# Causal attention and top-1 MoE on one core: the V loads of the first group are put at later places in the load queue

## The chip, the cores and the metric

The kernel runs on one NeuronCore of a Trainium2 chip. The metric is the device time of one execution in microseconds. The median of three runs of the kernel before is 532.28 us (532.24 to 537.39). The engines named below are TensorE (PE in the rows, PEld for its weight loads), VectorE (DVE), ScalarE (ACT), GpSimd (POOL) and SyncE (SP), which here issues all the loads that matter.

## What is computed

Attention with a memory over B=4, H=8, S=576, D=64, then a mixture of experts with one expert for each token (2304 tokens of 512, 8 experts, hidden size 1024).

```python
scores = np.where(causal, -1e9, q @ k.T / sqrt(D))
local  = softmax(scores) @ v
mem    = einsum('bhsd,bhde->bhse', phi(q), M_prev) / (phi(q) . z_prev + 1e-06)
x      = g * mem + (1 - g) * local            # g = sigmoid(beta), x is 2304 x 512
e      = argmax(normalize(x) @ normalize(expert_emb).T / tau)
out    = gate * (relu(x @ w1[e]) @ w2[e])
```

## The kernel before

**Tiling.** The attention is done in 8 groups: batch b and one half of the heads (4 heads), group 0 being batch 0, heads 0 to 3. The 576 rows of a group are four full tiles of 128 and a tail of 64, so there are query tiles i = 0 to 4 and key blocks 0 to 4 (the last one is the tail). Query tile i reads the key blocks 0 to i. A query tile of a group is worked in units of one or more heads: scores on TensorE (L692), maximum and mask on VectorE (L703), exponent on ScalarE (L731), transposes of the result on TensorE (L740) into the tiles aT0 to aT3 by a copy (L752, L754), then the product with V on TensorE (L767, function sC). Ahead of the scores stand the transposes of q and k (L604, L563, L634) and their split into two parts (L613, L622). L852 multiplies phi(q) with the memory, whose matrices M and normalisers z are loaded into Mb (L534, L535). Fillers (L272) are matmuls on an identity that the kernel places in waits of TensorE.

The second half is the mixture of experts: L1505 is its first product, L1518 transposes the hidden values, L1522 (ScalarE) and L1526 (VectorE) split them, L1532 is the second product, L1545 moves its result. L1491 transposes gathered rows of x and L1495 moves them. L1358 to L1371 load weights.

**What sets the order.** Nearly all work is handed to a list scheduler (class Sched) as operations with a name, an engine, a modelled duration, the operations that it depends on, and a priority; a lower number goes first. The scheduler plays the engines and the DMA transfers in modelled time and picks on each engine, among operations that can start at about the same modelled time, the one with the lowest priority number. The program is written in the order of the modelled starts, and on the chip each engine runs its list in order. Real waits come from semaphores that are derived from the tiles which an instruction reads and writes, so an instruction waits for all that it touches, whether or not the scheduler's list of dependences has it.

**The loads.** All loads of q, k, V, M and z are issued by SP in one queue. q and k of group 0 have the priorities 0.3 n for tile n (k 0.1 lower, the tail counts as n = 4), those of group 1 1.5 (k 1.4), M and z of batch 0 1.2. Each tile of q, k or V is one load of 128 rows by 4 heads by 64 floats, 131,072 bytes; a tail is half of that. The V rows of group 0 go into the tile VN0, one load for each key block (function load_v, L519, operation `("lv", 0, n)`). VN is a tile of [128, 5 blocks, 4 heads, 65]: 64 values and a one for each head. Its constant parts are written by POOL (L322 to L324).

**The product with V.** For the query tiles 0 to 3, sC takes for each head 128 columns from the flat tile:

```python
c = VW * kb + (D + 1) * hh
nc.tensor.matmul(
    lt[:, P * hh : P * hh + P], u["aT"][:, P * y : P * y + P], vt[:, c : c + P], start=kb == 0, stop=kb == i
)
```

VW is 4 x 65 = 260 columns, a key block. The columns that head hh reads begin at 65 hh and are 128 wide; those behind the 65 of the head are not used afterwards. The list of dependences of this operation (L822 to L824) holds `("lv", gi, kb)` for kb up to i, and for i = 3 also block 4.

Of the kernel before, what the change touches and what calls it, by code (L numbers as in the profile page):

```python
# [39 lines left out]
class Sched:  # L40
# [12 lines left out]
    def op(self, name, eng, dur=0, fn=None, deps=(), prio=0.0, alloc=(), free=(), xfer=None, at=0.0, late=0):  # L53
        alts = eng if isinstance(eng, list) else [(eng, dur, fn)]
        o = dict(name=name, alts=alts, deps=deps, prio=prio, alloc=alloc, free=free, xfer=xfer, n=len(self.ops), at=at, late=late)
        assert name not in self.byname, name
        self.byname[name] = o
        self.ops.append(o)
        for key in free:
            self.nrel[key] = self.nrel.get(key, 0) + 1  # L60
# [115 lines left out]
def kernel(  # L176
# [21 lines left out]
    SP = S + P - TAIL  # L198
# [8 lines left out]
    cfg = PRIO  # L207
# [12 lines left out]
    op, SL = sc.op, sc.slot  # L220
# [80 lines left out]
    def ub(gi):  # L301
        return UB[max(gi, 0)]
# [208 lines left out]
    def load_v(gi):  # L511
        b, g = groups[gi]
        key = ("VN", gi)
        names = []
        for n in range(NFULL + 1):
            r = P if n < NFULL else TAIL

            def f(n=n, r=r):
                nc.sync.dma_start(  # L519
                    VN[SL[key]][0:r, n, :, 0:D], v[b, 4 * g : 4 * g + 4, P * n : P * n + r, :].rearrange("h p d -> p h d")  # L520
                )

            op(("lv", gi, n), "SP", 450, f, (("lva", gi),), (0.4 + 0.3 * n if gi == 0 else ub(gi - 1) + cfg.get("lv", 3.0)),
               xfer=728 * r // P)
        op(("lva", gi), "NOP", 0, None, (), (0.8 if gi == 0 else ub(gi - 1) + cfg.get("lv", 3.0)),
           alloc=(("VN", key),), at=0.0)
# [1117 lines left out]
    for gi in range(NG):  # L1644
        load_v(gi)
        prep_group(gi)
# [172 lines left out]
```

## Time and profile before

| what | us |
|---|---|
| median of the runs | 532.28 |
| the profiled execution | 533.08 |
| its span, first to last instruction | 531.4 |
| TensorE busy in the span | 509.9 (96%) |
| VectorE busy | 309.5 (58%) |
| ScalarE busy | 321.2 (60%) |
| TensorE idle from 0 to 35 us | 4.99 |

The span is 1.7 us shorter than the execution's time. The granted clock of TensorE is 0.995 of full speed on average. Times in the rows count from the start of the span. In a timeline a row is a run of like instructions: its start, the time from the start of its first to the end of its last one, the engine, the line, the operation, the tiles (out<-in), and in brackets the idle time of the engine before it with what ended it. "SPq" and "ACTq" are the queues of SP and ScalarE; a row of SPq is the issuing of a load, not its transfer. TensorE works through a float32 matmul in several passes, so the trace can count more instructions than the order shows. The table's last line is the sum of the idle parts of the seven 5-us windows up to 35 us.

### The profile page before, as it was taken

What the parts mean: (1) busy time and instruction counts of PE and PEld (TensorE: products, weight loads), DVE (VectorE), ACT (ScalarE), POOL (GpSimd) and SP (SyncE); (2) the same over time, 40 slices, a digit from 0 to 9 for tenths busy, and PEclk for the clock granted to TensorE, in tenths of its full rate; (3) what the DMA queues carried; (4) which work ended last, traced back from release to release, by engine and by line L of the source; (5) the groups of instructions that cost most, each with busy time, mean ns of one, the idle gap of its engine ahead of it and who ended that gap; (6) DMA issues with size and microseconds to landing.
All of it is one profiled execution on the core that took longest, in us unless ns stands there. A gap on an engine that the chain in (4) does not pass through costs nothing. (4 is left out here: it accounts for less than half of the span.)

```text
span 531.4 us, 11427 instructions
## 1 busy us (share of the span) xinstructions
PE 509.9 (96%) x3506; PEld 439.7 (83%) x3506; DVE 309.5 (58%) x1003; ACT 321.2 (60%) x627; POOL 191.6 (36%) x266
## 2 busy tenths in 40 slices
PE   7899999999999999999997999999999999999991
PEld 6789998898899999988775888888888888888871
DVE  5677787777877877788981223411157514554540
ACT  5787876678877877687622353532367535664550
POOL 7211524434433433348437222232233332223320
PEclk9999999999999999999999999999999999999997
DMA  6657845135642311376418837542268863787340
GB/s 156 144 79 160 188 102 129 34 82 127 141 108 47 81 41 41 80 264 155 99 13 241 279 85 218 166 114 60 61 218 259 247 174 92 254 292 202 80 79 19
DMA packets 127471, 71.94 MB, mean 135 GB/s; under 512 B 111384, under 2 KB 111512, under 8 KB 127394
## 3 DMA queue, kind: packets, MB, share of 16 engines
q1 hardware_dynamic: 122242, 59.49, 43.1%
q0 software_dynamic: 5152, 11.57, 7.2%
q8 instruction: 30, 0.49, 0.5%
q14 instruction: 47, 0.39, 0.3%
HBM read 111.74 MB, written 10.67 MB: 230 GB/s over the span
## 5 line engine op out<-in xcount | busy, mean ns | idle before, releaser
L1505 PE MATMUL aux<-RB 128*128 128x512 f32 x528 | 126.0, 391 | 3.8 <-ACTq L1457 2.9
L1532 PE MATMUL L<-RC,hhl 128*128 128x512 f32 x528 | 129.1, 394 | 0.1
L1505 PEld LDWEIGHTS aux<-RB 128*128 128x128 f32 x528 | 98.3, 188 | 24.9 <-ACTq L1457 3.1
L1532 PEld LDWEIGHTS L<-RC,hhl 128*128 128x128 f32 x528 | 97.5, 188 | 19.9 <-ACT RC L1389 0.5
L1526 DVE TENSOR_TENSOR hhl<-aux,hhl 128x512 fp32r<-128x512 f32 x45 | 30.9, 690 | 118.1 <-ACTq L1457 58.9
L767 PE MATMUL L<-VN,aT 128*128 128x128 f32 x640 | 87.3, 276 | 0.0
L767 PEld LDWEIGHTS L<-VN,aT 128*128 128x128 f32 x640 | 78.9, 191 | 2.0 <-DVE aT L754 1.1
L1522 ACT ACTIVATE hhl<-aux 128x512 fp32r<-128x512 f32 x45 | 26.7, 598 | 77.2 <-PE aux L1518 40.7
L703 DVE CUSTOM_DVE_ANT_0 a<-aux,mask 128x128 f32<-128x128 f32 (+3 forms) x144 | 62.3, 452 | 12.9 <-PE aux L692 7.9
L731 ACT ACTIVATE a<-a,nb 128x128 f32<-128x128 f32 (+3 forms) x128 | 65.2, 557 | 1.7 <-DVE nb L703 1.2
L740 PE MATMUL aux<-ident,a 128*128 128x128 f32 x384 | 61.8, 278 | 1.5 <-ACT a L731 1.4
L1442 POOL DMA_INDIRECT a<-x_dram,ix x26 | 29.9, 1152 | 85.0 <-DMA ix<-id_dram 72.2
L752 ACT ACTIVATE aT<-aux 128x512 f32<-128x512 f32 (+3 forms) x89 | 44.6, 513 | 26.3 <-PE aux L740 23.7
L919 POOL TENSOR_TENSOR A<-ms,dd 128x256 f32<-128x256 f32 x32 | 20.7, 646 | 90.0 <-DVE dd L903 55.5
L740 PEld LDWEIGHTS aux<-ident,a 128*128 128x128 f32 x384 | 43.5, 141 | 10.1 <-ACT a L731 3.5
L1558 POOL DMA_INDIRECT out_dram<-ys,ix x21 | 22.3, 1064 | 78.3 <-ACTq L1457 55.3
L1514 ACT ACTIVATE hs<-aux 128x512 f32<-128x512 f32 x44 | 23.9, 595 | 36.1 <-PE aux L1505 35.5
L1393 DVE TENSOR_TENSOR RB<-RA,RB 128x1024 fp32r<-128x1024 f32 x24 | 28.4, 1223 | 12.2 <-ACT RB L1389 10.8
L1393 DVE TENSOR_TENSOR RC<-RA,RC 128x1024 fp32r<-128x1024 f32 x24 | 28.5, 1224 | 5.2 <-ACT RC L1389 5.0
L1449 POOL DMA_INDIRECT gg<-gate_dram,ix x23 | 25.8, 1121 | 7.0 <-issue 7.0
L852 PE MATMUL aux<-Mb,qp 128*128 128x130 f32 x160 | 25.1, 279 | 1.9 <-DMA Mb<-in_z_prev_dram 1.9
L925 POOL TENSOR_TENSOR X<-A,Xl 128x256 f32<-128x256 f32 x32 | 24.3, 760 | 5.5 <-DVE Xl L913 2.9
(259 smaller groups left out, 764.2 us busy)
## 6 DMA issues: line engine op xcount, KB each, us to landing
RA<-in_moe_w_dram SPq DMA_DIRECT2D x78, 1024.0 KB
RA<-in_moe_w_dram SPq DMA_DIRECT2D x16, 512.0 KB
RA<-in_k_dram SPq DMA_DIRECT2D x32, 128.0 KB
RA<-in_q_dram SPq DMA_DIRECT2D x32, 128.0 KB
VN<-in_v_dram SPq DMA_DIRECT2D x32, 128.0 KB
x_dram<-x SPq DMA_DIRECT2D x16, 256.0 KB
RA<-in_k_dram SPq DMA_DIRECT2D x8, 64.0 KB
RA<-in_q_dram SPq DMA_DIRECT2D x8, 64.0 KB
```

Of the source, the lines that this page charges most:

```text
L703: nc.vector.tensor_tensor_reduce(out=o, in0=i0, in1=i1, op0=ALU.add, op1=ALU.min, scale=-0.125, scalar=init, accum_out=acc)
L731: nc.scalar.activation(out=a[:, c], in_=a[:, c], func=AF.Exp, scale=-1.0, bias=nb[:, y : y + 1])
L740: nc.tensor.transpose(ps[:, P * y : P * y + P], a[:, P * y : P * y + P], ident)
L752: nc.scalar.activation(out=u["aT"][0:r, o : o + n], in_=t[0:r, 0:n], func=AF.Copy)
L767: nc.tensor.matmul(lt[:, P * hh : P * hh + P], u["aT"][:, P * y : P * y + P], vt[:, c : c + P], start=kb == 0, stop=kb == i)
L1393: nc.vector.tensor_tensor(l, s, h.bitcast(F32), op=ALU.subtract)
L1442: nc.gpsimd.indirect_dma_start(out=xg, out_offset=None, in_=x_dram[0:rows, :], in_offset=bass.IndirectOffsetOnAxis(ap=ix[:, 0:1].bitcast(U ...
L1449: nc.gpsimd.indirect_dma_start(out=gg, out_offset=None, in_=gate_dram[:, :], in_offset=bass.IndirectOffsetOnAxis(ap=G[i]["ix"][:, 1:2].bit ...
L1505: nc.tensor.matmul(G[i]["hp"][n], a[:, cc], w[:, c, 512 * n : 512 * n + 512], start=c == 0 and a is xh and w is w1h, stop=c == KD - 1 and ...
L1522: nc.scalar.activation(out=big("hhl")[n][:, 0:512], in_=G[i]["gps", n], func=AF.Copy)
L1526: nc.vector.tensor_tensor(t[:, 512:1024], G[i]["gps", n], t[:, 0:512].bitcast(F32), op=ALU.subtract)
L1532: nc.tensor.matmul(G[i]["yp"], t[:, cc : cc + P], w[:, c, :], start=c == 0 and a == 0 and w is w2h, stop=c == KF - 1 and a == 1)
```

## The change

The priority of the V loads of group 0 goes from 0.4 + 0.3 n to 0.8 + 0.3 n; all other groups' are as before, and no other line differs.

```diff
-            op(("lv", gi, n), "SP", 450, f, (("lva", gi),), (0.4 + 0.3 * n if gi == 0 else ub(gi - 1) + cfg.get("lv", 3.0)),
+            op(("lv", gi, n), "SP", 450, f, (("lva", gi),), (0.8 + 0.3 * n if gi == 0 else ub(gi - 1) + cfg.get("lv", 3.0)),
                xfer=728 * r // P)
```

Since the scheduler's modelled times move with it, the order of all engines changes in places. On SP, at the start of the queue, the rows stood so before (VN0 is the V tile of group 0, RA holds q and k, bet is beta):

```order
4 L501 DMA RA_80<-in_k_dram 128x4x64
5 L501 DMA RA_80<-in_q_dram 128x4x64
6 L519 DMA VN0_86<-in_v_dram 128x4x64
7 L501 DMA RA_80<-in_k_dram 128x4x64
8 L501 DMA RA_80<-in_q_dram 128x4x64
9 L519 DMA VN0_86<-in_v_dram 128x4x64
10 L501 DMA RA_80<-in_k_dram 128x4x64
11 L501 DMA RA_80<-in_q_dram 128x4x64
12 L519 DMA VN0_86<-in_v_dram 128x4x64
13 L501 DMA RA_80<-in_k_dram 128x4x64
```

and in the changed kernel:

```order
4 L501 DMA RA_80<-in_k_dram 128x4x64
5 L501 DMA RA_80<-in_q_dram 128x4x64
6 L501 DMA RA_80<-in_k_dram 128x4x64
7 L501 DMA RA_80<-in_q_dram 128x4x64
8 L501 DMA RA_80<-in_k_dram 128x4x64
9 L519 DMA VN0_86<-in_v_dram 128x4x64
10 L501 DMA RA_80<-in_q_dram 128x4x64
11 L501 DMA RA_80<-in_k_dram 64x4x64
12 L519 DMA VN0_86<-in_v_dram 128x4x64
13 L501 DMA RA_80<-in_k_dram 128x4x64
```

The first V load has moved from row 6 to row 9, the second from 9 to 12, and the third has left this stretch. Further down SP's queue, from the last load of z for batch 0 on, the changed kernel has these rows (a row with x4 is four loads; en and ta are the experts' embeddings and tau; the row with 64x4x64 ahead of an x4 is the tail of group 1):

```order
21 L535 DMA Mb0_93<-in_z_prev_dram 64x4x1
22 L501 DMA RA_80<-in_k_dram 128x4x64
23 L501 DMA RA_80<-in_q_dram 128x4x64
24 L451 DMA en_145<-in_moe_expert_emb_dram 8x512
25 L452 DMA ta_147<-in_moe_tau_dram 128x1
26 L501 DMA RA_80<-in_k_dram 128x4x64
27 L501 DMA RA_80<-in_q_dram 128x4x64
28 L501 DMA RA_80<-in_k_dram 64x4x64
29 L501 DMA RA_80<-in_k_dram 128x4x64 x4
30 L519 DMA VN0_86<-in_v_dram 128x4x64
31 L501 DMA RA_80<-in_q_dram 64x4x64
32 L501 DMA RA_80<-in_q_dram 128x4x64 x4
```

Row 30 is the third V load, the rows 33 and 34 behind these the fourth and the tail. Before, the last load of z was row 22, the fourth V load row 27, group 1's q tail row 32 and the V tail row 34.

On TensorE, around L852 of group 0, the rows stood so before (L_439 is the result tile of query tile 1 of group 0, VN0 its V, aT2 and aT3 the transposed scores of its two units, each of two heads and two key blocks):

```order
118 L852 MATMUL aux_431<-Mb0_93,qp0_84 128x130 x2
119 L767 MATMUL L_439<-VN0_86,aT2_91 128x128 x4
120 L740 MATMUL aux_451<-ident_71,a_377 128x128 x4
121 L740 MATMUL aux_460<-ident_71,a_399 128x128 x3
122 L740 MATMUL aux_469<-ident_71,a_423 128x128 x3
123 L852 MATMUL aux_479<-Mb0_93,qp0_84 128x130 x2
124 L740 MATMUL aux_485<-ident_71,a_434 128x128 x3
125 L767 MATMUL L_439<-VN0_86,aT3_92 128x128 x4
126 L563 MATMUL aux_509<-ident_71,RA_80 128x64 x4
```

and in the changed kernel, where the result tile is L_441:

```order
112 L852 MATMUL aux_425<-Mb0_93,qp0_84 128x130 x2
113 L740 MATMUL aux_433<-ident_71,a_376 128x128 x4
114 L767 MATMUL L_441<-VN0_86,aT2_91 128x128 x4
115 L740 MATMUL aux_456<-ident_71,a_399 128x128 x3
116 L740 MATMUL aux_462<-ident_71,a_419 128x128 x3
117 L767 MATMUL L_441<-VN0_86,aT3_92 128x128 x4
118 L563 MATMUL aux_484<-ident_71,RA_80 128x64 x4
119 L852 MATMUL aux_491<-Mb0_93,qp0_84 128x130 x2
120 L740 MATMUL aux_499<-ident_71,a_430 128x128 x3
```

The second product of query tile 1 with V (aT3) has moved ahead of the second L852 and of three L740. Ahead of the fourth k and q tile's L604 there were 16, 8, 3 and 6 fillers; now there are 16, 8 and 6.

On TensorE at the place where the attention's last work has ended and the experts' products go on, before the gathered rows (a) are first transposed by L1491, the rows stood so before:

```order
869 L1532 MATMUL L<-RC,hhl 128x512 x18
870 L1505 MATMUL aux<-RB 128x512 x12
871 L1518 MATMUL aux<-ident,hs 128x128 x8
872 L1505 MATMUL aux<-RB 128x512 x12
873 L1532 MATMUL L<-RC,hhl 128x512 x24
874 L1505 MATMUL aux<-RB 128x512 x6
875 L1491 LDWEIGHTS a
```

and in the changed kernel, where eight fillers (L272) stand ahead of the first of these rows and L1532 x18 and L1505 x6 ahead of the fillers:

```order
880 L272 MATMUL aux<-ident_76 128x128
881 L1518 MATMUL aux<-ident,hs 128x128 x8
882 L1505 MATMUL aux<-RB 128x512 x6
883 L1532 MATMUL L<-RC,hhl 128x512 x24
884 L1505 MATMUL aux<-RB 128x512 x18
885 L1491 LDWEIGHTS a
```

Six of the L1505 ahead of L1518 and six of those behind it have moved: six stand ahead of L1518 now, six behind it, and eighteen behind L1532. The aux tiles of the six behind L1518 are in the changed order the PSUM banks that L1518 wrote.

## Rows read from the trace of the kernel before

**Rows 1.** Busy us by stretch (instructions), TensorE's granted clock, DMA share, GB/s

```profile
5.00:10.00 5.00, 4.88 (x47) 3.85 (x46) 2.98 (x11) 2.92 (x8) 4.44 (x25) 1.00 0.82 185
10.00:15.00 5.00, 4.84 (x40) 3.82 (x40) 4.70 (x21) 4.66 (x14) 1.49 (x13) 1.00 0.69 147
15.00:20.00 5.00, 3.07 (x28) 2.64 (x27) 1.23 (x6) 2.68 (x7) 0.00 (x0) 1.00 0.65 140
35.00:240.00 205.00, 204.93 (x1874) 185.82 (x1873) 160.04 (x665) 158.74 (x363) 79.79 (x110) 1.00 0.45 108
```

**Rows 2.** TensorE's longest waits: us in total, times, longest

```profile
PE aux L1505 <- ACTq L1457: 2.9, 1, 2.9
PE aux L272 <- DVE ident L230: 2.5, 1, 2.5
PE aux L852 <- DMA Mb<-in_z_prev_dram: 1.9, 1, 1.9
```

**Rows 3.** SP's longest wait from 0 to 45 us

```profile
SPq L519 <- POOL VN L324: 1.2, 1, 1.2
```

**Rows 4.** Timeline of SP, 0 to 34 us

```profile
1.87 0.50 SPq L404 DMA_DIRECT2D bet<-in_beta_dram  x1
...
2.89 0.51 SPq L501 DMA_DIRECT2D RA<-in_q_dram  x1
4.61 0.37 SPq L519 DMA_DIRECT2D VN<-in_v_dram  x1
...
12.14 0.60 SPq L534 DMA_DIRECT2D Mb<-in_M_prev_dram  x1
...
13.45 1.46 SPq L534 DMA_DIRECT2D Mb<-in_M_prev_dram  x1
14.95 0.62 SPq L535 DMA_DIRECT2D Mb<-in_z_prev_dram  x1
...
22.38 3.33 SPq L501 DMA_DIRECT2D RA<-in_q_dram  x5
```

**Rows 5.** Timeline of TensorE, 12 to 34 us

```profile
12.85 0.71 PE L767 MATMUL L<-VN,aT 128*128 128x128 f32 x4
...
14.38 1.50 PE L692 MATMUL aux<-RB 64*128 64x384 f32 x12
17.80 0.69 PE L852 MATMUL aux<-Mb,qp 128*128 128x130 f32 x4 [1.93 <-DMA Mb<-in_z_prev_dram]
18.33 1.05 PE L767 MATMUL L<-VN,aT 128*128 128x128 f32 x8
19.22 1.26 PE L740 MATMUL aux<-ident,a 128*128 128x128 f32 x10
20.48 0.71 PE L852 MATMUL aux<-Mb,qp 128*128 128x130 f32 x4
21.03 0.49 PE L740 MATMUL aux<-ident,a 128*128 128x128 f32 x3
...
22.34 0.46 PE L563 MATMUL aux<-ident,RA 64*128 64x64 f32 x4
```

**Rows 6.** Timeline of ScalarE: the first use of beta

```profile
4.55 0.21 ACT L338 ACTIVATE invg<-bet 128x8 f32<-128x8 f32 x1 [2.45 <-DMA bet<-in_beta_dram]
```

**Rows 7.** Timeline of all engines, 268 to 290 us

```profile
272.50 1.66 PE L1505 MATMUL aux<-RB 128*128 128x512 f32 x6 [0.46 <-ACT hs L1514]
...
273.99 1.03 PE L1518 MATMUL aux<-ident,hs 128*128 128x128 f32 x8
274.63 1.09 ACT L1522 ACTIVATE hhl<-aux 128x512 fp32r<-128x512 f32 x2 [1.69 <-PE aux L1518]
...
275.26 0.69 DVE L1526 TENSOR_TENSOR hhl<-aux,hhl 128x512 fp32r<-128x512 f32 x1 [2.02 <-ACT hhl L1522]
...
284.42 0.62 PE L1491 MATMUL aux<-ident,a 128*128 128x128 f16 x8
...
286.81 0.60 ACT L1495 ACTIVATE RB<-aux 128x512 fp32r<-128x512 f16 x1 [2.40 <-remote]
```

## The prediction

> **What bounds the kernel now.** I read the busy time by stretch first. From 35 to 240 us TensorE is busy 204.93 of 205 us [rows 1]: whatever comes late before 35 us is carried to the end, and nothing in that stretch can be saved by earlier loads. So only places where TensorE stands still can gain or lose. The list of TensorE's waits names them [rows 2]: 2.5 us for the identity at the start, which no load touches, 1.9 us in front of L852 for the memory normaliser z, 2.9 us near 288 us. The one SP wait that the diff can touch is 1.2 us: the first V load stands behind the memset of VN by POOL (L324), and all loads stand behind it [rows 3].
>
> The queue of SP then shows how tightly the start is packed [rows 4]. The first V load begins at 4.61, the first M load at 12.14, the last z load at 14.95, the tail of group 1's q at 22.38. TensorE's own rows [rows 5] show that it ends twelve L692 at 15.88 (14.38 + 1.50) and starts L852 at 17.80, which is the 1.93 us.
>
> **The change part by part.** SP's order: V block 0 goes from sixth to ninth place, block 1 from ninth to twelfth, block 2 from twelfth to behind the k loads of group 1, block 3 and the tail behind its q loads.
>
> 1. *The wait for the memset goes.* k2 and q2 now stand where V0 was. q1 starts at 2.89 [rows 4], so the next starts at about 3.4 and V0 at about 5.1, after the memset: 1.2 us of queue are won.
>
> 2. *z comes earlier.* Before, 13 loads (V0 to the tail of group 0's q) take 4.61 to 12.14, 0.58 each; two loads ahead of them take 1.87 to 2.89, 0.51 each [rows 4]. After, 12 loads lie between q1 and M, so M starts at 3.4 + 12 x 0.58 = 10.4 (9.5 with 0.51). Then M, z, M, z: before, the last z started 2.81 behind the first M, of which the second M took 1.46; no row says why, so without its excess the step is 1.95. The last z: 11.5 to 13.2, I take 12.6. From issue to use z took 17.80 - 14.95 = 2.85 us, so L852 may go at 14.4 to 16.1, and TensorE gets there at about 15.9. The 1.93 us go, all but 0.2 at worst. **Taken alone: minus 1.9.**
>
> 3. *V block 2 comes too late.* L767 reads 128 columns of V for each head at a pitch of 65, so the fourth head reaches 63 columns into the next key block. The last of the four L767 with aT3 in the changed order (tile L_441) therefore reads V block 2, though query tile 1 multiplies only key blocks 0 and 1. The scheduler's dependences have block 2 only for query tile 2. Before, block 2 was the twelfth load and no L767 waited. After, it is the twelfth load behind the last z. Before, thirteen loads behind the last z took 14.95 to 22.38 [rows 4], so twelve are 6.86 us: V2 starts at 12.6 + 6.86 = 19.5 (18.4 to 20.1).
> Issue to use has no row for V at this place. The nearest: beta's took 4.55 - 1.87 = 2.68 us [rows 4, 6] and z's 2.85, both small; 131,072 bytes at the 185 GB/s of 5 to 10 us [rows 1] add 0.7 at most. So 2.7 to 3.5; I take 3.0, nearer the small ones, because the DMA engines were only 0.65 busy at 15 to 20 us [rows 1]. V2 can be used at 22.5 (21.1 to 23.6).
> When does TensorE want it? The trace counts eight L767 and four L852 where the order has four and two. From 15.9, by [rows 5]: L852 0.53 (17.80 to 18.33), four L740 0.50 (1.26 for ten), L767 0.89 (18.33 to 19.22), six L740 0.76, three quarters of the next L767 0.67: 19.25. **TensorE stands 3.2 us (1.8 to 4.3) where it stood 1.93 before.**
> The balance is made at one common point, the end of this L767 group: 22.34 before, with the second L852 (0.55) and three L740 (0.33) of the rows at 20.48 and 21.03 already done; after, these two come behind it. Loss = 22.5 + 0.25 (the last quarter) + 0.88 - 22.34 = **+1.3 us** (-0.1 to +2.4). Step 2's gain is already in it.
> The Trainium skill, DMA: Bandwidth & Descriptors, section "Anatomy of one DMA", gives 2.0 us plus bytes over 436 GB/s for a DMA of the gpsimd path. By that an estimate for V2 is 2.3 us, 0.7 less than mine, and the loss would be 0.6. The trace does not agree: z needed 2.85 us for 1 KB in all, from SP.
>
> 4. *V blocks 0, 1, 3 and the tail.* V0 starts at 5.1 instead of 4.61 and V1 three loads later, at 6.8; with 3.5 us both are there before 10.5, and the first L767 began at 12.85 [rows 5]. V3 starts six loads behind V2, at 22.9, and is there before 26.5; what reads it first stands some forty matmuls behind V2's reader, over 4 us by the means of [rows 5], so after 26.6. Covered, if narrowly; if not, a few tenths, which the range of step 3 holds. Nothing.
>
> 5. *Fewer fillers.* Ahead of the fourth k and q tile 33 filler matmuls become 30. TensorE's list has no wait there that they would fill or cause [rows 2]. Nothing.
>
> 6. *The order near 272 us.* The scheduler's modelled times shift, and one late choice flips (last pair of order rows): six L1505 that stood ahead of the L1518 transposes now stand behind L1532 x24, with eight fillers in their place, and the six behind L1518 write PSUM banks that hold L1518's results, so they wait until ACT (L1522) and DVE (L1526) have read them. By [rows 7]: before, TensorE is idle 0.46 up to 272.50; the fillers take this time. L1518 then takes 272.5 to 273.3 (its step to the next row is 0.79 = 274.78 - 273.99). ACT begins 0.64 behind L1518's start, DVE 0.63 behind ACT and takes 0.69: 272.5 + 1.96 = 274.5. TensorE idles about 1.2 us there and 0.46 less ahead of it, but that 0.46 goes to fillers: L1491, which began at 284.42, comes 1.2 us later. Yet the next matmul waits for ACT's L1495, which began at 286.81, 1.77 us after L1491's end (284.42 + 0.62), for no work that the trace names. If that start is fixed by something else, the 1.2 is absorbed; if it hangs on L1491, it is lost whole, and a second wait for the other bank adds up to 0.7. Bounds: 0 (a gain would need L1495 earlier, and nothing moves towards that) to +1.9; near the middle but lower, since 1.77 idle us can hold 1.2, I take **+0.5**.
>
> Sum: +1.3 + 0.5 = +1.8 us. On the profiled execution (533.08) that is 534.9. It lies 0.8 above the median of the runs, 532.28, and on that the sum is **534.1 us**.
>
> **Rivals.**
> A. *V2 in time* (the faster side): TensorE does not wait for V2, only z's 1.93 us go, and the late place costs 0.5 or nothing: 530.9 or 530.4. It decides at 19.25 for V2's use, so at a start of 16.5 with the shortest 2.7, that is twelve loads behind a z at 11.5 at 0.42 each. No pair of [rows 4] is that close, the nearest is 0.51: 7 in 100.
> B. *The stalls swap evenly.* With the 0.51 pitch and without the long M the start costs 0 to 0.3, and L1495 absorbs the late place: 532.3, give or take 0.6. For it: each is within the bounds above. Against it: the pitch of 0.58 held over 13 loads. 20 in 100.
> C. *Much is late.* V2 at 23.6 and the late place in full, +2.4 and 1.2 to 1.9: 535.9 to 536.6. A new wait would come on top in the ramp, where ACT and DVE are busy 4.66 and 4.70 of 5 us at 10 to 15 us [rows 1] and have their work in another order; at 1 to 1.5 us it gives about 538. 11 in 100, 4 of them beyond 1%.
> My forecast, 532.9 to 535.8, has the other 62.
>
> **Range.** 531.0 to 536.2 holds the forecast, B, and a part of A and C. About 1%, 5.3 us, is what a measurement of this kernel can tell from no change. Faster by that would need 527, more than all that z's wait and the late place could give: 0.02. Slower by that, the far end of C: 0.04. The same: 0.94.
>
> **What would show it.** In the list of TensorE's waits L852 for z is gone (step 2 is wrong if more than 0.3 is left) and L767 for the DMA of VN stands in its place, 1.8 to 4.3 us near 19 us (step 3 is wrong under 1). SP's wait on POOL is gone, the last z starts at 11.5 to 13.2 and V2 at 18.4 to 20.1. Near 273.5 L1505 waits about 1.2 us for DVE's L1526; if L1495 then starts at 286.8 plus only what the start lost, the late place was absorbed. A new wait of L692 or L740 for ACT or DVE between 10 and 35 us would be case C. A shorter span with no L767 wait is rival A.

## The result, and the profile after

The changed kernel takes 540.22 us (median of four runs, 539.59 to 541.63), the kernel before 533.15 in the runs beside it: a ratio of 1.0123, 95% interval 1.0088 to 1.0158. It is slower by about 1.2%, and the time lies 4 us above the range. Run again on other occasions the same kernel came to 1.0069 (1.0050 to 1.0089) and 1.0066 (1.0040 to 1.0093) of the kernel before, so the loss is between 0.7 and 1.2%, 3.5 to 7 us, and in each case more than the 1.8 us that were forecast. The kernel before itself lay between 531.3 and 539.5 us over all occasions, which is why only ratios of runs side by side are used below.

| | before | after |
|---|---|---|
| profiled execution | 533.08 | 541.63 |
| its span | 531.4 | 539.8 |
| TensorE busy | 509.9 | 515.7 |
| granted clock, mean | 0.995 | 0.982 |

TensorE's list of waits in the changed kernel (us in total, times, longest; it answers to [rows 2]):

```profile
PE L L767 <- DMA VN<-in_v_dram: 3.2, 1, 3.2
PE aux L272 <- DVE ident L230: 3.0, 1, 3.0
PE aux L1505 <- ACTq L1457: 3.0, 1, 3.0
PE aux L740 <- ACT a L731: 1.4, 1, 1.4
PE aux L1505 <- DVE hhl L1526: 1.0, 1, 1.0
```

L852 is gone from it, L767 for V and L1505 for L1526 have come. SP's rows at the places of [rows 4]:

```profile
5.16 0.44 SPq L519 DMA_DIRECT2D VN<-in_v_dram  x1
...
10.65 0.61 SPq L534 DMA_DIRECT2D Mb<-in_M_prev_dram  x1
...
12.62 0.61 SPq L535 DMA_DIRECT2D Mb<-in_z_prev_dram  x1
...
16.41 3.97 SPq L501 DMA_DIRECT2D RA<-in_k_dram  x5
20.43 0.51 SPq L519 DMA_DIRECT2D VN<-in_v_dram  x1
```

and TensorE's at the places of [rows 5]:

```profile
16.59 0.71 PE L852 MATMUL aux<-Mb,qp 128*128 128x130 f32 x4
...
19.13 0.83 PE L767 MATMUL L<-VN,aT 128*128 128x128 f32 x6
23.15 0.79 PE L767 MATMUL L<-VN,aT 128*128 128x128 f32 x2 [3.19 <-DMA VN<-in_v_dram]
23.87 0.69 PE L563 MATMUL aux<-ident,RA 64*128 64x64 f32 x4
...
26.29 1.65 PE L692 MATMUL aux<-RB 64*128 64x512 f32 x6
...
29.39 0.83 PE L767 MATMUL L<-VN,aT 128*128 128x128 f32 x6
```

The last quarter of the L767 group waits 3.19 us for V block 2. What was not foreseen is behind it. TensorE by windows of 1 us (length, TensorE's busy time and count, granted clock, DMA share, GB/s):

```profile
20.00:21.00 1.00, 0.00 (x0) 1.00 0.39 89
...
22.00:23.00 1.00, 0.00 (x0) 0.75 0.73 167
23.00:24.00 1.00, 0.85 (x3) 0.50 0.89 202
...
28.00:29.00 1.00, 1.00 (x6) 0.50 0.36 58
29.00:30.00 1.00, 1.00 (x9) 0.83 0.37 77
30.00:31.00 1.00, 1.00 (x11) 1.00 0.70 212
```

The granted clock is at 0.50, the 1.2 GHz level, from about 22.5 to 29.3 us, and TensorE, which has work again at 23.15, does it at half speed: six or seven matmuls in each us where it does eleven at 2.4 GHz. L692 x6 takes 1.65 us, against 0.96 where the clock is at 1.00 (the row of q_fill below).

Where the 8.4 us of the two spans arise, by marks that both kernels have (start of the first such instruction; from the timelines):

| mark | before | after | difference |
|---|---|---|---|
| first L692 | 7.23 | 8.06 | +0.8 |
| SP's first weight load, L1360 | 219.84 | 225.41 | +5.6 |
| ScalarE's first L1298, which needs those weights | 224.47 | 230.41 | +5.9 |
| L1224 | 266.29 | 272.40 | +6.1 |
| L1491 | 284.42 | 291.82 | +7.4 |
| the L1505 behind it | 287.92 | 295.39 | +7.5 |
| end | 531.4 | 539.8 | +8.4 |

So 5.6 us arise ahead of 220 us, 0.5 from there to L1224, 1.3 between L1224 and L1491, and 0.9 behind 295 us, where the clock was at half once more, in this execution, after the wait of 3.0 us for L1457. The window of 5 us there, all engines (length; busy time and count of TensorE's matmuls, its weight loads, VectorE, ScalarE and GpSimd; granted clock, DMA share, GB/s):

```profile
295.00:300.00 5.00, 4.61 (x14) 3.38 (x15) 1.11 (x2) 1.60 (x3) 2.61 (x4) 0.66 1.08 272
```

### The profile page after: what moved, and what is told of

It reads as the page before. It is cut to its first block, busy times and chain, and to the rows that moved or that the text cites. A ratio compares the mean times of both kernels' runs of the same rounds, so it can differ in the third digit from the quotient of the medians.

```text
span 539.8 us, 11448 instructions
## 1 busy us (share of the span) xinstructions
PE 515.7 (96%) x3511; PEld 443.5 (82%) x3511; DVE 309.7 (57%) x1003; ACT 321.9 (60%) x627; POOL 190.5 (35%) x266
## 5 line engine op out<-in xcount | busy, mean ns | idle before, releaser
L1505 PE MATMUL aux<-RB 128*128 128x512 f32 x528 | 127.1, 395 | 4.0 <-ACTq L1457 3.0
L1532 PE MATMUL L<-RC,hhl 128*128 128x512 f32 x528 | 129.1, 394 | 0.1
L1505 PEld LDWEIGHTS aux<-RB 128*128 128x128 f32 x528 | 99.4, 190 | 25.3 <-ACTq L1457 3.1
L1532 PEld LDWEIGHTS L<-RC,hhl 128*128 128x128 f32 x528 | 97.4, 188 | 19.9 <-ACT RC L1389 0.5
L1526 DVE TENSOR_TENSOR hhl<-aux,hhl 128x512 fp32r<-128x512 f32 x45 | 30.9, 689 | 119.2 <-ACT hhl L1522 60.2
L767 PE MATMUL L<-VN,aT 128*128 128x128 f32 x640 | 88.4, 277 | 3.2 <-DMA VN<-in_v_dram 3.2
L767 PEld LDWEIGHTS L<-VN,aT 128*128 128x128 f32 x640 | 79.3, 192 | 6.2 <-DMA VN<-in_v_dram 3.4
L740 PE MATMUL aux<-ident,a 128*128 128x128 f32 x384 | 62.9, 280 | 2.1 <-ACT a L731 1.4
L740 PEld LDWEIGHTS aux<-ident,a 128*128 128x128 f32 x384 | 44.2, 142 | 11.1 <-ACT a L731 4.4
L852 PE MATMUL aux<-Mb,qp 128*128 128x130 f32 x160 | 26.3, 288 | 0.0
```

What stands on the lines that cost most here:

```text
L740: nc.tensor.transpose(ps[:, P * y : P * y + P], a[:, P * y : P * y + P], ident)
L767: nc.tensor.matmul(lt[:, P * hh : P * hh + P], u["aT"][:, P * y : P * y + P], vt[:, c : c + P], start=kb == 0, stop=kb == i)
L852: nc.tensor.matmul(m[:, 130 * x : 130 * x + 130], qp[:, x, P * i - rr.start : P * i - rr.start + P], Mb[b % 2][:, 2 * g + x, :], start=Tru ...
L1505: nc.tensor.matmul(G[i]["hp"][n], a[:, cc], w[:, c, 512 * n : 512 * n + 512], start=c == 0 and a is xh and w is w1h, stop=c == KD - 1 and ...
L1526: nc.vector.tensor_tensor(t[:, 512:1024], G[i]["gps", n], t[:, 0:512].bitcast(F32), op=ALU.subtract)
L1532: nc.tensor.matmul(G[i]["yp"], t[:, cc : cc + P], w[:, c, :], start=c == 0 and a == 0 and w is w2h, stop=c == KF - 1 and a == 1)
```

## Experiments

Theory 1 is that the late V block 2 is the loss: its wait, and the half-speed clock behind that wait. Theory 2 is that the loss lies in the changed order of the other engines. The late place near 280 us is a third cause of known place. In most of the kernels one load is moved in the list of operations after the scheduler has done its work; the orders of all other engines then stay as they were. The move is this line, with other names in the other kernels:

```diff
-        order.sort(key=lambda o: o["start"])
+        order.sort(key=lambda o: o["start"]); o = next(o for o in order if o["name"] == ('lv', 0, 2)); order.remove(o); order.insert(1 + next(n for n, x in enumerate(order) if x["name"] == ('lv', 0, 1)), o)
```

All ratios are to the kernel before, run beside it ("changed" is the changed kernel, "before" the kernel before, with that edit):

| kernel | what differs | median us | ratio, 95% interval |
|---|---|---|---|
| a_v2_early | changed, V2 behind V1 | 536.86 | 1.0000 (0.9977 to 1.0024) |
| b_v2_late | before, V2 late | 543.79 | 1.0122 (1.0063 to 1.0182) |
| c_fill | changed (see below) | 542.14 | 1.0105 (1.0044 to 1.0166) |
| d_dep | changed, dependence told | 552.40 | 1.0302 (1.0263 to 1.0342) |
| e_fill | changed, fillers | 536.85 | 1.0064 (1.0044 to 1.0083) |
| f_place | changed, late place back | 537.81 | 1.0078 (1.0056 to 1.0100) |
| g_early_place | changed, V2 early, place back | 532.63 | 0.9998 (0.9977 to 1.0019) |
| h_v2_mid | changed, V2 two loads earlier | 537.27 | 1.0075 (1.0033 to 1.0118) |
| m_v2_near | changed, V2 four loads earlier | 536.72 | 1.0035 (1.0020 to 1.0050) |
| n_v0_only | before, V0 and V1 later | 533.90 | 1.0000 (0.9977 to 1.0024) |
| i_z_early | before, M and z earlier | 534.39 | 0.9999 (0.9984 to 1.0014) |
| k_again | changed | 538.61 | 1.0069 (1.0050 to 1.0089) |
| q_again | changed | 539.90 | 1.0066 (1.0040 to 1.0093) |
| q_fill | as e_fill | 539.25 | 1.0066 (1.0040 to 1.0092) |
| q_early | as a_v2_early | 533.94 | 0.9971 (0.9945 to 0.9997) |
| q_fill_place | e_fill and f_place | 540.02 | 1.0073 (1.0043 to 1.0103) |

a to d ran on one occasion, e to h on a second, i, k, m, n on a third, the q kernels on a fourth.

**a_v2_early.** The line above in the changed kernel.

> The changed kernel, with one load moved on SP: V block 2 directly behind V block 1; the order on all other engines is that of the changed kernel. Theory 1 (the late block 2 costs its wait of 3.2 us and then the half-speed clock from 22.5 to 29.2 us, about 3 us more): no wait of L767 for VN, granted clock 1.00 in every window up to 240 us, 540.2 - 6 = about 534. Theory 2 (the loss lies in the changed order of the ramp, the V2 wait only replaces the z wait): about 539 to 540, with new waits of L692 or L740 in the place of that of L767.

Measured: 1.0000, where the changed kernel itself (c_fill below) was at 1.0105 on the same occasion. The clock and the waits fit theory 1: no wait of L767, granted clock 1.00 in the windows from 15 to 35 us. The whole loss is gone with one load, though every other engine still runs the changed order. So the changed order is not the loss; what z's gain is worth is left to the later runs. The traces place the loss. L852 starts at 16.59 here as in the changed kernel, and the L767 group that starts at 29.39 there starts at 23.54 here, 5.85 us earlier. SP's first weight load is at 219.58 against 225.41, 5.83 earlier. In these two executions the loss ahead of 220 us is therefore complete by 29.4 us: it is the wait and the slow stretch behind it. q_early below repeats it.

**b_v2_late.** The same line in the kernel before, with ('lqk', 1, 0, 4) for ('lv', 0, 1).

> The kernel before, with one load moved on SP: V block 2 behind the tail of group 1's q; the order on all other engines is that of before. Theory 1: V2 can be used at about 25.4, TensorE wants it at about 22, so a wait of L767 of about 3 us, and after it the clock at half speed as in the changed kernel: 533 + 3 + 3 = about 538 to 539 (535.5 if the clock holds). Theory 2: nothing is lost beyond 1 us, 533 to 534.

Measured: 1.0122. The wait of L852 for z is gone here too. The wait of L767 was longer than expected, 4.3 us, and the clock behind it was at 0.50 in every window of 1 us from 24 to 30 us. A late V2 alone costs the kernel before as much as the whole change did.

**c_fill.** Fillers ahead of the four L767, but for a unit that starts with head 2; the second unit of query tile 1 starts with head 1, so none was issued and this is the changed kernel once more.

> The changed kernel with 40 filler matmuls (identity, 128 columns, 0.06 us each) ahead of the four L767 that wait for V block 2, so that TensorE works for about 2.5 of the 3.2 us; the data still come late. Theory 1 with the clock as the second half of the loss: wait of L767 at most 0.8 us, granted clock 1.00 from 20 to 30 us, 540.2 - 3 = about 537. Rival (the slow stretch behind the wait has another cause, e.g. late operands of ACT and DVE): 540, clock again at 0.5 or long waits.

Measured: 1.0105, wait 3.2 us. It tells something all the same: here the slow stretch began later, at 25.1, and ended at 28.5. In the four profiles of this kernel the wait is 3.2, 3.2, 3.1 and 4.1 us; the stretch behind it is twice as long in the first as in the other three.

**d_dep.** The missing dependence is told to the scheduler:

```diff
-        if i == 3:
-            pv += (("lv", gi, 4),)
+        if i < 4 and u["hs"][-1] == 3:
+            pv += (("lv", gi, i + 1),)
```

> The changed kernel with the missing dependence told to the scheduler (the last unit of query tiles 0 to 3 depends on the V load of the next block). The scheduler then puts that product with V behind later work, and the order changes in many places behind it. Theory 1: no wait of L767 for VN, no half-speed stretch at 20 to 30 us; the z wait of before is gone too; 532 to 535, depending on the late place. Theory 2: 538 to 540.

Measured: 1.0302, the slowest of all; the expectation for the time failed. The wait of L767 is gone as expected. But the scheduler's list flipped at the end of the attention:

```profile
PE L L1532 <- DVE RC L1312: 10.3, 1, 10.3
PE aux L1505 <- remote: 2.8, 1, 2.8
```

TensorE stands 10.3 us for the weights' split on VectorE (L1312) near 275 us, and the clock is at 0.50 to 0.56 from 270 to 285 (means of windows of 5 us). A right dependence in the list is no gain by itself: each edit of this list redraws the program behind it.

**e_fill.** 45 fillers into the result columns that the four L767 then overwrite, directly ahead of them:

```diff
-        lt, vn, vt = Lc[gi, i], VN[SL["VN", gi]], VNt[SL["VN", gi]]
+        lt, vn, vt = Lc[gi, i], VN[SL["VN", gi]], VNt[SL["VN", gi]]; [nc.tensor.matmul(lt[:, P : 2 * P], ident16, ident16, start=True, stop=True) for _ in range(45 if (gi, i, u["hs"][0]) == (0, 1, 1) else 0)]
```

> The changed kernel with 45 filler matmuls (identity, 128 columns, about 0.06 us each) directly ahead of the four L767 that wait for V block 2, so that TensorE works through most of the 3.2 us; the data still come at the same time. Theory 1 (stall and the half-speed clock behind it are two separate losses): wait of L767 at most 0.8 us, granted clock 1.00 from 20 to 30 us, about 3 us less than the changed kernel, so 1.004 to 1.008 of the kernel before. Rival (what follows the stall is slow for another reason): no gain, 1.010 to 1.013 of before, windows from 23 to 29 us as slow as in the changed kernel.

Measured: 1.0064, no wait, clock 1.00 from 20 to 35 us. That is as expected, but the profiled execution had a slow start (last section): TensorE came to the fillers only at 21.94, against 19.96 to the wait in the changed kernel, so that the missing wait is not the work of the fillers alone. And k_again and q_again, without fillers, came to nearly the same ratio on other occasions, so it had to be repeated beside them (q_fill).

**f_place.** One dependence puts the late place back as it was before:

```diff
-                op(("ehT", i, n), "PE", 4 * e_pe, lambda i=i, n=n: e_T(i, n, bank(("eg", i, n))), (("ere", i, n),), pp + 3,
+                op(("ehT", i, n), "PE", 4 * e_pe, lambda i=i, n=n: e_T(i, n, bank(("eg", i, n))), (("ere", i, n),) + ((("el1", -1, 0),) if i == -2 else ()), pp + 3,
```

> The changed kernel with only the late place put back: six L1505 stand ahead of L1518 again, so that no L1505 waits for L1526 (V block 2 stays late; fourteen fillers stand in that gap). If the late place costs 1.2 us that nothing absorbs: 1.2 us less than the changed kernel, 1.009 to 1.010 of before; the wait of L1505 for DVE L1526 is gone and L1491 comes 1.2 us earlier against the L1532 ahead of it. If it is absorbed by the start of L1495: same as the changed kernel.

Measured: 1.0078, and the trace resolves it better than the time. TensorE's timeline of the kernel before at L1224 (its L1491 is in [rows 7]):

```profile
266.29 0.18 PE L1224 MATMUL aux<-cum,ones 128*128 128x8 f16 x1
```

The same of the changed kernel, to L1491:

```profile
272.40 0.18 PE L1224 MATMUL aux<-cum,ones 128*128 128x8 f16 x1
...
280.80 1.66 PE L1505 MATMUL aux<-RB 128*128 128x512 f32 x6 [0.97 <-DVE hhl L1526]
...
291.82 0.62 PE L1491 MATMUL aux<-ident,a 128*128 128x128 f16 x8
```

And of f_place, from the L1532 behind its L1224:

```profile
274.12 4.35 PE L1532 MATMUL L<-RC,hhl 128*128 128x512 f32 x18
...
292.54 0.62 PE L1491 MATMUL aux<-ident,a 128*128 128x128 f16 x8
```

From L1224 to L1491 it is 18.13 us before and 19.42 after. From the L1532 x18, which starts 0.04 behind L1224 (272.44 after), it is 19.38 after and 18.42 in f_place. So the place costs 1.29 us in the traces, of which f_place takes back 0.96; its fillers, which take longer than the idle time that they fill, account for the rest.

**g_early_place.** a_v2_early and f_place together.

> The changed kernel with V block 2 directly behind V block 1 and the late place put back. Theory 1: the gain at z (1.9 us) is left and both losses are gone: 1.5 us less than the kernel before, 0.996 to 0.998 of it. Theory 2 (other order changes cost as much as z gives): 0.999 to 1.002.

Measured: 0.9998. Both losses are gone, but so is z's gain; theory 2's numbers were met here. i_z_early and n_v0_only show where such a gain can go.

**h_v2_mid and m_v2_near.** V2 behind the second of group 1's full k tiles, and behind its k tail, four loads earlier than in the change.

> The changed kernel with V block 2 two loads earlier (behind the second of group 1's full k tiles), so that it comes about 1.1 to 1.6 us earlier: wait of L767 about 1.6 to 2.1 us instead of 3.2, which is about the length of the z wait of before, behind which the clock stayed at 1.00. Theory 1 with the half-speed stretch as a consequence of a long stand: clock 1.00 at 20 to 30 us, and the kernel is 1.5 + 3 us faster than the changed one, 1.002 to 1.006 of before. Rival (each us of lateness costs the same, no step): 1.5 us faster only, 1.008 to 1.010.

> The changed kernel with V block 2 four loads earlier, behind group 1's k tail: it starts at about 17, can be used at about 20.1, and L767 waits about 0.9 us. If the half-speed stretch needs a longer stand: clock 1.00 from 20 to 30 us, 1.001 to 1.004 of before. Rival (any wait there brings it): 1.005 to 1.009 with the clock at 0.5.

TensorE's row of the wait in h:

```profile
21.83 0.79 PE L767 MATMUL L<-VN,aT 128*128 128x128 f32 x2 [2.42 <-DMA VN<-in_v_dram]
```

Its windows of 1 us, columns as above:

```profile
21.00:22.00 1.00, 0.17 (x1) 0.72 0.87 196
22.00:23.00 1.00, 1.00 (x6) 0.50 0.79 179
...
27.00:28.00 1.00, 1.00 (x7) 0.50 0.34 43
28.00:29.00 1.00, 1.00 (x10) 0.87 0.37 66
```

and the row of the wait in m:

```profile
20.52 0.49 PE L767 MATMUL L<-VN,aT 128*128 128x128 f32 x2 [0.68 <-DMA VN<-in_v_dram]
```

h stood 2.4 us and lost as much as the changed kernel on the two later occasions (1.0075 against 1.0069 and 1.0066; the changed kernel did not run beside it), with a slow stretch as long as that in the first profile of the changed kernel; my expectation that the clock would hold failed. m stood 0.7 us, its clock stayed at 1.00, and it came to 1.0035. So a stand costs more than its length once the clock falls behind it. Its length alone does not tell whether the clock falls. Behind the waits for V2 of 2.4 us and more it fell in all seven profiles. But it also fell behind stands at other places of 1.5 (q_early, near 289 us), 1.7 (i_z_early, near 228 us) and 1.9 us (c_fill, near 232 us), and it stayed at 1.00 behind z's 1.93 us and the 2.9 us of [rows 2], and behind 2.5 and 2.8 us near 228 and 234 us in n_v0_only and k_again.

**n_v0_only and i_z_early.** Two parts of what the change does well, in the kernel before: V0 behind the fourth k load and V1 behind the k tail; and M and z of batch 0 behind the third V load.

> The kernel before with a part of the change alone, on SP only: V block 0 behind the fourth k load and block 1 behind the k tail; blocks 2, 3 and the tail stay where they were, and so does the order on all other engines. SP's wait for POOL goes and z starts 1.2 us earlier: wait of L852 about 0.7 instead of 1.9, about 1.2 us faster, 0.997 to 0.999 of before. Rival (the load queue gives the 1.2 us back): wait of L852 still 1.5 to 1.9.

> The kernel before with only M and z of batch 0 moved on SP, ahead of the six loads that stood between the third V load and them; the order on all other engines is that of before. If the 1.9 us in front of L852 are carried to the end and nothing else is late: the last z starts at about 11.2, no wait of L852, 1.5 to 1.9 us faster, 0.9965 to 0.997 of before. Rival (a later wait takes them up, or the six delayed loads are missed): 0.999 to 1.001.

Neither has any wait of L852 left, and neither is faster: 1.0000 and 0.9999. So the 1.93 us that TensorE stands for z are real in the trace of [rows 5] and were worth nothing in the end on this occasion. In i_z_early L852 starts at 16.62 instead of 17.80; 0.42 us go again to a wait of L634 for a q load, one of those that had been moved back, and by the L774 near 220 us nothing is left (219.69 against 219.62). In n_v0_only L852 starts at 16.96, and 0.77 us are left at that L774 (218.85). What is left there ends at the first load of expert weights. Its use by ScalarE, from the timelines; in the kernel before:

```profile
224.47 1.06 ACT L1298 ACTIVATE RB<-RA 128x1024 fp32r<-128x1024 f32 x1 [1.55 <-DMA RA<-in_moe_w_dram]
```

In i_z_early:

```profile
226.14 1.06 ACT L1298 ACTIVATE RB<-RA 128x1024 fp32r<-128x1024 f32 x1 [3.15 <-DMA RA<-in_moe_w_dram]
```

In n_v0_only:

```profile
226.15 1.06 ACT L1298 ACTIVATE RB<-RA 128x1024 fp32r<-128x1024 f32 x1 [4.00 <-DMA RA<-in_moe_w_dram]
```

In k_again:

```profile
231.44 1.06 ACT L1298 ACTIVATE RB<-RA 128x1024 fp32r<-128x1024 f32 x1 [4.27 <-DMA RA<-in_moe_w_dram]
```

SP issued these loads at 219.84, 219.77, 218.93 and 223.95, so they took 4.6, 6.4, 7.2 and 7.5 us. ScalarE stands for them, and in the last three TensorE then stands for ScalarE (L740, 1.7, 2.5 and 2.8 us near 228 to 234 us). In i_z_early the clock then falls as well, which lengthens the loss. TensorE's row of that stand:

```profile
228.38 0.55 PE L740 MATMUL aux<-ident,a 128*128 128x128 f32 x3 [1.67 <-ACT a L731]
```

ScalarE's window of 2 us behind it, whose column behind the bracket is TensorE's granted clock:

```profile
230.00:232.00 2.00, 1.42 (x2) 0.50 1.09 351
```

A us won earlier is lost here when the load takes its longer time; in the profile of before it took the shortest time of all. This was seen in one execution of each kernel; that it explains the whole of the two ratios is argued, not shown.

**k_again and the four q kernels.** The changed kernel as it is, and, beside it, fillers, early V2, and fillers with the late place back.

> The changed kernel again, unaltered, beside the others on one chip. Theory 1: 1.010 to 1.013 of before with a wait of L767 of 3.2 us and, in most executions, a half-speed stretch of 3 to 7 us behind it; an execution whose clock holds is about 3 us shorter.

> The changed kernel, unaltered, as the measure for the three that follow on the same chip. Expected: 1.007 to 1.012 of the kernel before.

> The changed kernel with 45 fillers ahead of the four L767 that wait for V block 2. If the half-speed stretch behind the stand is a loss of its own: granted clock 1.00 from 20 to 30 us and 1.5 to 3 us less than the changed kernel of the same chip (a slow stretch of 3 to 6 us, half of it lost). If the fillers only move the time: the same as the changed kernel within 0.1%.

> The changed kernel with V block 2 directly behind V block 1. If the late block is the whole loss but for the late place: 3.5 to 6 us less than the changed kernel of the same chip (the stand of 3.2 and the slow stretch), 0.999 to 1.002 of before. If order changes elsewhere carry the loss: within 1 us of the changed kernel.

> The changed kernel with the 45 fillers and with the late place put back. If the late place is a loss that adds to the others: 0.9 to 1.3 us less than with the fillers alone. If something near 290 us absorbs it: the same as with the fillers alone.

k_again and q_again confirm the loss, at its smaller size. q_early is 5.96 us below q_again (533.94 against 539.90): with block 2 early the change costs nothing, and as far as the medians resolve it this is the whole of its loss. The two traces say the same: the L767 group at 29.05 in q_again starts 5.63 earlier in q_early, and the first weight load is 5.64 earlier. q_early's row:

```profile
23.42 0.83 PE L767 MATMUL L<-VN,aT 128*128 128x128 f32 x6
```

q_again's profiled wait was 4.1 us, so some 1.6 to 1.9 us come on top of the wait. q_early is even at 0.9971 of the kernel before, just clear of 1. In the trace q_fill does what was expected, the clock holds (TensorE's timeline):

```profile
19.01 2.68 PE L763 MATMUL L<-ident 128*128 128x128 f16 x45
21.52 0.89 PE L767 MATMUL L<-VN,aT 128*128 128x128 f32 x6
22.85 0.49 PE L767 MATMUL L<-VN,aT 128*128 128x128 f32 x2 [0.44 <-DMA VN<-in_v_dram]
...
24.63 0.96 PE L692 MATMUL aux<-RB 64*128 64x512 f32 x6
...
26.69 0.83 PE L767 MATMUL L<-VN,aT 128*128 128x128 f32 x6
```

From the last quarter of this L767 to the next L767 group it is 3.84 us here (22.85 to 26.69), 6.24 in the changed kernel (23.15 to 29.39), for the same instructions: 2.4 us for the clock alone in that execution. In q_again the same stretch is 24.02 to 29.05, 5.03, so 1.2 us. But the median of q_fill is only 0.65 us below that of q_again, with intervals that lie on each other: the expectation of 1.5 to 3 us failed. Part is plain: V2 is as late as ever, and the wait is most of the loss. The traces show more. q_fill is 2.35 us ahead of q_again at the first weight load (222.72 against 225.07) and still 2.57 ahead at the L1505 behind L1457 (292.67 against 295.24), so here nothing is lost at the weights. Behind that L1505 the clock of q_fill falls, that of q_again does not, and at the end q_fill is 1.1 us ahead (spans of 537.2 and 538.3). TensorE's window of 5 us of q_fill there, columns as above:

```profile
295.00:300.00 5.00, 5.00 (x22) 0.75 1.08 281
```

Whether this is why the medians hardly differ is open: it is one execution of each, and that the half speed behind V2's wait costs the median anything is shown by no run by itself. q_fill_place is no faster than q_fill, 540.02 against 539.25, and its profile still has a wait of 1.4 us for V2: 1 us is below what these runs resolve (535.1 to 543.8), and only the trace shows the late place.

## Why the prediction was wrong

*Steps 1 and 2 came as forecast.* SP's wait for POOL is gone, V0 starts at 5.16 (5.1), the last z at 12.62 (12.6), and L852 does not wait.

*Step 3 had the wait right and its price wrong.* V2 started at 20.43, a little past the range of 18.4 to 20.1, because the five k loads ahead of it took 3.97 us; it could be used 2.72 us later (2.7 to 3.5). TensorE came at 19.96 instead of 19.25. Wait: 3.19 against 3.2. That they agree to 0.01 us is luck: both ends came 0.7 us late, and other profiles of the kernel have 3.1 to 4.1. The step that failed is the balance at the common point: it counted the work behind the wait at the durations of [rows 5], that is at 2.4 GHz. In the profiled execution the balance came to +3.3 instead of +1.3: V2 was usable 0.65 later than forecast, and the last quarter, the second L852 and the three L740 took 1.4 us more at 1.2 GHz. Another 1.0 us of half speed fell behind that point, 2.4 in all. No rival had it. The timeline of the kernel before could have raised it: the 16 fillers at the start, TensorE's first work after standing, take 0.12 us each, against 0.06 for the 45 of q_fill.

```profile
2.45 1.89 PE L272 MATMUL aux<-ident 128*128 128x128 f16 x16 [2.45 <-DVE ident L230]
```

I read [rows 2] only for lengths of waits.

The Trainium skill, TensorE: Matmul & The Clock Gate, section "HAM oscillation — how this bites in real kernels", describes a kernel whose matmuls start cold again after each wait for a DMA. The traces here agree: behind the waits for V2 of 2.4 to 4.3 us the clock was at 0.50 for 3 to 7 us in every profile of the changed kernel and in b, f and h. Other stands of 1.5 to 2.9 us were followed by half speed in some profiles and not in others. A wait that an edit lengthens wants that term beside its length, as a chance.

*Also in step 3, the gain at z was counted in full.* n_v0_only, i_z_early and g_early_place say that it is worth nothing in the median; q_early, at 0.9971, leaves room for some of it. If it is nothing, the term was not -1.9 + 3.2 but nearer to 0 + 3.2 + the clock, 4.4 to 5.6 with 1.2 to 2.4 us for the clock. That is within what was measured (3.5 to 7 us). The late place would add 1.3; the times do not show it, since a_v2_early and q_early have it and lose nothing. How the median loss divides into wait, clock and z is argued from the traces, not shown by the times.

*Step 4 came as forecast:* no wait for the blocks 0, 1, 3 and the tail. *Step 5 too.*

*Step 6 had the mechanism and the size, and the wrong share.* L1505 waits for L1526 for 0.97 us, and L1491 comes 1.29 us later (1.2 forecast). I took 0.5, supposing that L1495's unexplained start would absorb the rest. It does not: the wait of L1505 for L1457 is 2.9 before and 3.0 after, and it varied from 1.1 to 4.2 over the other profiles, with the late place and without it. It differs by execution, and no run shows that it absorbs the place; in the profile after it did not (+7.4 at L1491, +7.5 at the L1505 behind it).

*The range* was narrower than the unknowns: the upper end left out a clock that falls, and the forecast rested on one profiled execution of before that had the shortest start, the shortest first load of weights and no slow stretch. The chance of 0.04 for slower by over 1% was too small by far.

*The rival C* ("much is late") had the right side, and two of its terms were near: V2 usable at 23.15 where it had 23.6, and the late place in full. Its third was wrong: no new wait came in the ramp, and the half speed stands in its place.

## What to carry to other kernels

An instruction waits for all that it touches: where a matmul reads past the columns it needs, ask which load fills those, before moving that load. Price a new wait of TensorE twice, by its length and by the half-speed work that may follow it, and look up in the timeline what work after a stand costs. A wait that disappears is worth its length only if nothing later takes the time back; the next fixed point, here a later q load and then the first load of the weights, has to be asked first.

## What the runs showed of the hardware

TensorE's durations at the start are those of half speed, and for how long differs by execution, though the granted clock reads 1.00 there. The first two groups of twelve L692 took 0.88 and 0.98 us before and 1.25 and 0.97 in the changed kernel. TensorE's timeline of e_fill:

```profile
8.07 1.54 PE L692 MATMUL aux<-RB 64*128 64x128 f32 x12
...
10.59 1.65 PE L692 MATMUL aux<-RB 64*128 64x256 f32 x12
12.17 0.82 PE L272 MATMUL aux<-ident 128*128 128x128 f16 x6
...
14.52 1.32 PE L692 MATMUL aux<-RB 64*128 64x384 f32 x6
```

Six L692 of 384 columns take 0.82 us in the changed kernel. In e_fill the half speed lasted until about 15 us and cost 2.8 us at L852 (19.40 against 16.59). The durations show it, the clock column does not.

The first load of expert weights moves little for its first us. ScalarE's windows of 2 us in k_again, whose last two columns are the DMA engines' share and GB/s:

```profile
224.00:226.00 2.00, 1.26 (x4) 1.00 1.11 25
226.00:228.00 2.00, 0.77 (x2) 1.00 0.59 41
228.00:230.00 2.00, 0.00 (x0) 1.00 0.42 158
230.00:232.00 2.00, 0.56 (x1) 1.00 1.02 391
```

The engines are busy at 25 to 41 GB/s for about 4 us, then move 391; before, the slow part was 2 us long. No run here tells why.

The same cast of the identity by VectorE (L230) took 0.97 us in some executions and 1.55 in others, which TensorE's first instruction follows (2.45 and 3.03 us); the changed kernel's 0.58 us there is such a case, since i_z_early, made from the kernel before, has it too.
